# Loading q, and the first two batches of k, as rows of eight tokens, in a kernel of windowed attention followed by an expert layer

## The chip, the cores and the metric

The kernel runs on one core of a Trainium2 chip. The metric is the device time of one execution in microseconds (us); less is better. Granted TensorE clock, the share of full speed that the profile shows, is given where it is not near 1. Times of different series come from different chips, so the time of an experiment is compared only with runs of the kernel before on the same chip in the same rounds. Of the kernel before only one profile was kept, so starts and stages in the experiments' profiles are set against that one, across chips.

In the lines of the profile PE is TensorE, PEld its weight loads, DVE VectorE, ACT ScalarE, POOL GpSimd and SP SyncE; L304 is line 304 of that kernel; the span runs from the start to the end of the profiled execution.

## The reference

Attention over 8 batches of 8 heads, 576 tokens, head size 64. A token sees the tokens at most 32 away and 8 global tokens; the global tokens see and are seen by all. Its output goes through a two-matrix layer with a sine activation, called "expert layer" here.

```python
scores = scale * np.matmul(q, k.transpose(0, 1, 3, 2))          # [8, 8, 576, 576]
mask = np.abs(pos[:, None] - pos[None, :]) <= 32
mask = mask | is_global[:, None] | is_global[None, :]
attn = softmax(np.where(mask, scores, -1e9))                     # cut: written out
x = np.matmul(attn, v).transpose(0, 2, 1, 3).reshape(4608, 512)

h = x @ w_in                                                     # [4608, 2048]
s = np.sin(alpha * h)
out = (h + s * s / (alpha + 1e-09)) @ w_out                      # [4608, 512]
```

## The kernel before

All work of a batch is one attention stage and one expert stage; in the steady state the second half of the expert layer of batch b-1 fills the attention stage of batch b, and the loads of batch b+1 are issued there too. Batch 0 has nothing to be overlapped with: its attention is the *front* of the program.

Loads of q, k and v and of the weights are issued by GpSimd, which casts to bf16 on the way. One load of q or k is one head (the first two batches, `split`) or one tile of 96 tokens; a piece of it is one token of one head, 64 elements, 256 bytes in DRAM and 128 bytes as bf16.

```python
def load_slots(b, split):
    QS = qkp.tile([TW, NTW, H, D], BF, name="QS")     # 96 x 6 x 8 x 64
    KS = qkp.tile([TW, NTW, H, D], BF, name="KS")
    ...                                                # cut: by_head, by_tile, v_rows
    f = by_head if split else by_tile
    kq = [partial(f, src, dst, i) for i in range(H if split else NTW)
          for src, dst in ((k, KS), (q, QS))]
    ...
    return kq[:4] + vs + kq[4:] if split else kq + vs
```

Both are transposed two heads at a time on TensorE into PSUM (six transposes of 96 columns each), and copied out: k by VectorE, laid out window by window (overlapping windows, 1344 elements per partition), q by ScalarE.

The front also needs small things: the rows of the global tokens (`gN`, gathered by SyncE's and ScalarE's queues, k first, then q, then v), a copy of global v into the buffer of v (`VgN` to `VW`), and the vector alpha, brought with its elements spread over the partitions.

The start of the main program, in order:

```python
stage_T(0, 0, psA, "qp"); globals_all(); ...; stage_T(0, 1, psA, "qp")
globals_v_all()                        # cast of global v, then the reciprocal
shift_v(0)                             # SyncE: shifted copies of v
global_v(0)                            # SyncE: VW<-VgN, waits for the cast
parts, last = attention(0, psA, {2: 0, 3: 2})
with_extra(parts, w_loads, 3, 2)       # GpSimd: 8 weight loads, 2 per attention step
parts[3] = partial(chain, parts[3], pool_regs)
late = load_slots(1, True)             # issued in batch 0's expert stage
```

GpSimd takes a weight load when it comes to it.

The softmax here doesn't subtract the row's maximum and nothing guards it: scores larger than these inputs give would overflow.

## Time and profile before

| | before |
|---|---|
| time, median of 3 runs | 385.82 us (385.81 to 385.98) |
| span of the profiled run, granted clock | 385.0 us, 0.996 |
| first attention output matmul (`num`) | 29.27 us |
| first expert matmul (`hb`) of batch 0 / batch 1 | 46.29 / 90.68 us |
| between later batches | 37.97 to 38.48 us |

The page of the profile of before, from the slices of the span (one digit is the busy tenths of 9.6 us), the packet count and the shares of the chain that ended last:

```profile
PE   1128499798999999999999999999999999999796
DVE  7725459574977497649774976497749774954500
...
DMA packets 133723, 35.31 MB, mean 92 GB/s; under 512 B 123314, under 2 KB 128178, under 8 KB 133682
...
PE 52%; ACT 18%; DVE 10%; issue 7%; POOL 7%; DMA 3%; POOLq 1%; ACTq 0%; DVEq 0%
```

From the ninth slice on TensorE is the limit (8 or 9 tenths nearly to the end). In the first five it is not: there TensorE is at 1, 1, 2, 8, 4 tenths and something else holds the program. The stage table of before confirms this. Its columns are the stretch, its length, then busy us (and instructions) of PE, PEld, DVE, ACT and POOL, then the granted clock, the DMA share in tenths and GB/s; the stretches run from one batch's first `hb` matmul to the next one's, for batches 0, 1 and 4:

```profile
46.29:90.68 44.39, 39.97 (x385) 18.53 (x385) 28.59 (x73) 32.83 (x57) 23.88 (x44) 1.00 1.07 106
90.68:128.80 38.12, 37.41 (x384) 18.14 (x384) 26.90 (x64) 32.51 (x57) 31.20 (x53) 1.00 1.65 136
205.63:243.60 37.97, 37.15 (x385) 18.05 (x384) 26.63 (x59) 29.58 (x50) 31.28 (x48) 1.00 0.94 98
```

A steady batch is 37 us of TensorE in 38 us. Batch 0's stage has 4.4 us of TensorE idle time, the front far more.

The timeline of the front in before, VectorE first. Columns: start, length, engine, line, operation, out<-in, shapes, count, and in brackets the idle time before it and what ended that:

```profile
19.99 0.41 DVE L278 CAST VgN<-gN 64x512 bf16<-64x512 f32 x1
25.36 0.25 DVE L279 RECIPROCAL recipT<-alphaT 128x16 f32<-128x16 f32 x1 [4.96 <-DMA alphaT<-in_moe_alpha_dram]
25.52 0.86 DVE L344 TENSOR_TENSOR E<-E,MASK 128x672 bf16<-128x672 bf16 x2
```

The same stretch on TensorE:

```profile
18.54 0.64 PE L304 MATMUL Kps<-identb,KS 96*128 96x96 bf16 x6 [2.27 <-DMA KS<-in_k_dram]
...
29.27 0.58 PE L375 MATMUL num<-E,VW 128*64 128x56 bf16 x12 [2.36 <-DMA VW<-VgN]
...
46.29 16.56 PE L457 MATMUL hb<-xT,w_in 128*128 128x512 bf16 x64 [3.36 <-POOL xT L402]
```

And on GpSimd, the issue of the weights:

```profile
21.79 0.78 POOL L532 DMA_DIRECT2D w_in<-in_moe_w_in_dram  x1 [0.36 <-DMA KS<-in_k_dram]
25.82 0.74 POOL L532 DMA_DIRECT2D w_in<-in_moe_w_in_dram  x1 [3.25 <-DMA QS<-in_q_dram]
32.13 1.49 POOL L532 DMA_DIRECT2D w_in<-in_moe_w_in_dram  x2 [5.56 <-issue]
33.60 2.98 POOL L532 DMA_DIRECT2D w_out<-in_moe_w_out_dram  x4
```

VectorE stands 4.96 us on alphaT and only then does the first mask product, although its input was finished on ScalarE at 22.76. TensorE then still waits for global v (2.36 us). The first weight load is issued at 21.79, and the second only at 25.82, after 3.25 us in which it waits for q's loads.

The groups by form, with busy time, mean ns of one, and idle time before, for the two copies that the change turns into strided ones:

```profile
L310 DVE COPY kTw<-Kps 128x1344 bf16<-128x1344 bf16 x32 | 27.1, 848 | 1.9 <-PE Kps L304 1.9
L324 ACT COPY qT<-qp 128x576 bf16<-128x576 bf16 x20 | 12.7, 633 | 18.4 <-PE ops L268 13.2 <-PE qp L319 5.1
```

### The profile page before, as it was taken

The numbers are of one execution on the slowest core, as the hardware profiler recorded it, in microseconds if no ns is written. First come the engines' busy times: TensorE is split into PE (matmuls) and PEld (weight loads), VectorE is DVE, ScalarE is ACT, GpSimd is POOL, SyncE is SP. The second block draws the span as 40 slices with busy tenths as digits, with TensorE's granted clock in tenths as the row PEclk, the third lists the DMA queues.
The fourth block names the chain that finished last, engine by engine and source line by source line (L and its number), as shares of the span: only waits on it lengthen the run. The fifth ranks groups of instructions, "written<-read, shape, count | busy, mean of one in ns | idle before, by whom it ended". The sixth has DMA issues, their size and how long they took to land.

```text
span 385.0 us, 8609 instructions
## 1 busy us (share of the span) xinstructions
PE 336.2 (87%) x3208; PEld 162.9 (42%) x3208; DVE 244.9 (64%) x551; ACT 258.4 (67%) x435; POOL 249.3 (65%) x394
## 2 busy tenths in 40 slices
PE   1128499798999999999999999999999999999796
PEld 0015244443444444444544444444444444344342
DVE  7725459574977497649774976497749774954500
ACT  1057487786988588858885888578857885744310
POOL 8934396227878589858986898689768006854400
PEclk9999999999999999999999999999999999999989
DMA  6999999257999409940994099409940001000012
GB/s 53 136 162 161 190 164 165 37 77 77 155 132 153 124 9 103 148 127 7 103 148 126 7 103 149 128 6 113 137 128 5 30 30 54 2 28 27 29 54 82
DMA packets 133723, 35.31 MB, mean 92 GB/s; under 512 B 123314, under 2 KB 128178, under 8 KB 133682
## 3 DMA queue, kind: packets, MB, share of 16 engines
q0 software_dynamic: 122560, 19.02, 69.4%
q1 hardware_dynamic: 8034, 15.54, 13.9%
q10 hardware_dynamic: 3088, 0.21, 0.8%
q8 instruction: 25, 0.41, 0.4%
q14 instruction: 16, 0.13, 0.1%
HBM read 38.42 MB, written 9.44 MB: 124 GB/s over the span
## 4 chain that ended last, share of the span: by engine, by line
PE 52%; ACT 18%; DVE 10%; issue 7%; POOL 7%; DMA 3%; POOLq 1%; ACTq 0%; DVEq 0%
PE hb L457 22%; PE ops L494 13%; PE o L494 8%; ACT Sb L464 6%; ACT E L342 4%; DMA KS<-in_k_dram 3%; DVE H2b L447 3%; PE num L375 3%; ACT S L470 2%; DVE S L472 2%; DVE kTw L310 2%; ACT lnd L358 2%; PE hb L494 2%; ACT rec L360 2%; PE Sp L336 2%
## 5 line engine op out<-in xcount | busy, mean ns | idle before, releaser
L457 PE MATMUL hb<-xT,w_in 128*128 128x512 bf16 x576 | 133.1, 384 | 6.0 <-POOL xT L402 4.8
L464 ACT ACTIVATE Sb<-hb,alphaT 128x512 bf16<-128x512 f32 x144 | 96.6, 684 | 55.2 <-PE hb L457 53.9
L447 DVE SCALAR_TENSOR_TENSOR H2b<-S,recipT,hb 128x512 bf16<-128x512 bf16 x144 | 102.6, 741 | 29.3 <-POOL S L472 28.8
L472 POOL TENSOR_TENSOR S<-Sb 128x512 bf16<-128x512 bf16 x91 | 92.6, 1040 | 34.1 <-ACT Sb L464 31.5
L457 PEld LDWEIGHTS <-w_in 128*128 128x128 bf16 x576 | 56.5, 99 | 74.4 <-issue 10.9
L494 PE MATMUL ops<-w_out,H2b 128*128 128x512 bf16 x320 | 81.7, 385 | 3.2 <-DVE osb L502 3.0
L494 PEld LDWEIGHTS <-H2b 128*128 128x128 bf16 x576 | 50.6, 98 | 58.6 <-issue 7.3
L344 DVE TENSOR_TENSOR E<-E,MASK 128x672 bf16<-128x672 bf16 x64 | 34.1, 534 | 32.9 <-ACT E L342 32.2
L494 PE MATMUL o<-w_out,H2b 128*128 128x512 bf16 x224 | 54.7, 380 | 0.0
L342 ACT ACTIVATE E<-Sp 128x672 bf16<-128x672 f32 x64 | 45.9, 717 | 4.1 <-PE Sp L336 4.0
L402 POOL COPY xT<-xg 128x4 bf16 x64 | 12.9, 201 | 48.9 <-DVE xg L400 45.5
L107 POOL DMA_DIRECT2D VW<-in_v_dram x56 | 42.5, 776 | 0.7 <-issue 0.3
L358 ACT ACTIVATE lnd<-den 128x288 f32<-128x288 f32 x64 | 26.4, 412 | 18.3 <-PE den L352 17.8
L382 DVE TENSOR_TENSOR xT<-num,rec 128x288 bf16<-128x288 f32 x64 | 28.7, 449 | 6.1 <-PE num L375 4.8
L375 PEld LDWEIGHTS <-VW 128*64 128x64 bf16 x768 | 18.3, 116 | 33.1 <-DVE gn L386 10.9
L472 DVE TENSOR_TENSOR S<-Sb 128x512 bf16<-128x512 bf16 x30 | 18.3, 609 | 21.5 <-ACT Sb L464 20.6
L375 PE MATMUL num<-E,VW 128*64 128x56 bf16 x768 | 25.3, 201 | 6.9 <-DVE gn L386 3.1
L360 ACT ACTIVATE rec<-lnd 128x288 f32<-128x288 f32 x64 | 28.3, 443 | 2.0
L310 DVE COPY kTw<-Kps 128x1344 bf16<-128x1344 bf16 x32 | 27.1, 848 | 1.9 <-PE Kps L304 1.9
L336 PE MATMUL Sp<-qT,kTw 64*128 64x56 bf16 x768 | 22.1, 190 | 6.0 <-ACT E L342 4.1
L100 POOL DMA_DIRECT2D QS<-in_q_dram x30 | 23.2, 774 | 3.0 <-DMA QS<-in_q_dram 3.0
L324 ACT COPY qT<-qp 128x576 bf16<-128x576 bf16 x20 | 12.7, 633 | 18.4 <-PE ops L268 13.2
(73 smaller groups left out, 305.1 us busy)
## 6 DMA issues: line engine op xcount, KB each, us to landing
out_dram<-osb SPq DMA_DIRECT2D x36, 256.0 KB
VW<-in_v_dram POOLq DMA_DIRECT2D x40, 112.0 KB, 4.8
VW<-VW SPq DMA_DIRECT2D x8, 384.0 KB
KS<-in_k_dram POOLq DMA_DIRECT2D x30, 96.0 KB, 4.7
QS<-in_q_dram POOLq DMA_DIRECT2D x30, 96.0 KB, 4.7
w_in<-in_moe_w_in_dram POOLq DMA_DIRECT2D x4, 512.0 KB, 8.0
w_out<-in_moe_w_out_dram POOLq DMA_DIRECT2D x4, 512.0 KB, 13.1
VW<-VW SPq DMA_DIRECT2D x8, 240.0 KB
```

The source lines that it names most:

```text
L107: nc.gpsimd.dma_start(out=W[p0 : p0 + n, par, u, :].rearrange("p (h d) -> p h d", d=D), in_=v[b, :, key0 : key0 + n, :].rearrange("h p d - ...
L310: nc.vector.tensor_copy(out=kTw[hp][:, :, 0:KB], in_=bass.AP(tensor=base.tensor, offset=base.offset, ap=[list(base.ap[0]), [QB, NW], [1, KB]],
L342: nc.scalar.activation(out=E[:], in_=Sp[:, :, 0:EW], func=AF.Exp, scale=scale)
L344: nc.vector.tensor_tensor(out=E[:], in0=E[:], in1=mk[:, None, :].to_broadcast([P, 2, EW]), op=ALU.mult)
L358: nc.scalar.activation(out=lnd[:], in_=den[:, :, 0:QB], func=AF.Ln)
L360: nc.scalar.activation(out=rec[:], in_=lnd[:], func=AF.Exp, scale=-1.0)
L375: nc.tensor.matmul(out=num[pr, u, :], lhsT=W[:, i % 2, i // 2, c0 : c0 + 64], rhs=E[:, t, u * QC : (u + 1) * QC], start=True, stop=True, s ...
L447: nc.vector.scalar_tensor_tensor(out=H2b[:, n_, :], in0=s_[:], scalar=recipT[:, n_ : n_ + 1], in1=h_, op0=ALU.mult, op1=ALU.add,)
L457: nc.tensor.matmul(out=h2[:], lhsT=w_in[:, ci, nt * P : (nt + 1) * P], rhs=xT[:, ci, c * CH : (c + 1) * CH], start=(ci == 0), stop=(ci == ...
L464: nc.scalar.activation(out=Sb[:], in_=h2[:], func=AF.Sin, scale=alphaT[:, nt : nt + 1])
L472: eng.tensor_tensor(out=S2[:], in0=Sb[:], in1=Sb[:], op=ALU.mult)
L494: nc.tensor.matmul(out=ops[:], lhsT=H2b[:, nt, ts * P : (ts + 1) * P], rhs=w_out[:, nt, :], start=(nt == 0), stop=(nt == NT - 1),)
```

## The change

The intent: eight consecutive tokens of one head lie side by side in DRAM, 2 KB in one piece. If a partition takes eight tokens of one head, the loads have an eighth of the pieces and, with several heads per load, there are fewer loads to issue. The tokens then stand on 72 partitions, eight to a partition, so the transposes are of one head at a time (72 columns, 16 in place of 6), write tokens in the order "j, then partition", and the copies out of PSUM read with a stride to put them back. All q, and k of batches 0 and 1, go this way. With GpSimd freed of issues, half the squares of the first expert stage and all of the second's go to the later split, in which GpSimd does most of them.

```diff
-        QS = qkp.tile([TW, NTW, H, D], BF, name="QS")
-        KS = qkp.tile([TW, NTW, H, D], BF, name="KS")
+        QS = qkp.tile([TR, H, JR, D], BF, name="QS")                 # 72 x 8 x 8 x 64
+        KS = qkp.tile([TR, H, JR, D] if b < 2 else [TW, NTW, H, D], BF, name="KS")
...
-        f = by_head if split else by_tile
-        kq = [partial(f, src, dst, i) for i in range(H if split else NTW) for src, dst in ((k, KS), (q, QS))]
+        n_ = 2 if split else H
+        if b < 2:
+            kq = [partial(by_rows, src, dst, i, n_) for i in range(0, H, n_) for src, dst in ((k, KS), (q, QS))]
+        else:
+            kq = [partial(by_tile, k, KS, i) for i in range(NTW)] + [partial(by_rows, q, QS, 0, H)]
...
+        if b < 2:
+            for j in range(JR):
+                for t, pr in heads:
+                    nc.tensor.transpose(
+                        out=Kps[pr, j * RP + WR : j * RP + WR + TR],
+                        in_=KS[:, 2 * hp + t, j, :], identity=identb[0:TR, 0:TR])
+            nc.vector.tensor_copy(
+                out=kTw[hp][:, :, 0:KB].rearrange("p i (c j) -> p i c j", j=JR),
+                in_=kview([[QB // JR, NW], [1, KB // JR], [RP, JR]]))
...                                                    # q alike, in every batch
         nc.scalar.copy(
-            out=qT[hp][:, :, 0:QB], in_=Qps[:].rearrange("p (i c) -> p i c", c=QB)
+            out=qT[hp][:, :, 0:QB].rearrange("p i (c j) -> p i c j", j=JR),
+            in_=Qps[:].rearrange("p (j i c) -> p i c j", j=JR, c=QB // JR),
         )
...
+    sq_first = lambda nt: (sq_early if nt < 8 else sq_late)(nt)
...
-                        ld = load_slots(p + 1, p == 1)
+                        ld = load_slots(p + 1, False)
                         if p == 1:
-                            late = ld[5:]
-                            ld = ld[:5]
-                            with_extra(parts, ld, 6, 1)
+                            with_extra(parts, ld, 3, 2)
...
-            m1 = mm1(p, H2[p], psB, sq_early if p < 2 else sq_late)
+            m1 = mm1(p, H2[p], psB, sq_late if p else sq_first)
```

More of the change, by code (lines that the diff above doesn't have):

```diff
@@ L52 @@
     NTW = S // TW
+    JR = 8
+    TR = S // JR
+    WR = WIN // JR
+    RP = TR + 2 * WR
     CT = DM // P
@@ L88, in load_slots, with by_rows @@
     def load_slots(b, split):
-        QS = qkp.tile([TW, NTW, H, D], BF, name="QS")
-        KS = qkp.tile([TW, NTW, H, D], BF, name="KS")
+        QS = qkp.tile([TR, H, JR, D], BF, name="QS")
+        KS = qkp.tile([TR, H, JR, D] if b < 2 else [TW, NTW, H, D], BF, name="KS")
         qk[b] = (QS, KS)
         W = VW[b % 2]
-        def by_head(src, dst, h):
+        def by_rows(src, dst, h0, n):
             nc.gpsimd.dma_start(
-                out=dst[:, :, h, :], in_=src[b, h].rearrange("(t p) d -> p t d", p=TW)
+                out=dst[:, h0 : h0 + n, :, :].rearrange("p h j d -> p h (j d)"),
+                in_=src[b, h0 : h0 + n].rearrange("h (p j) d -> p h (j d)", j=JR),
             )
@@ L299, in globals_in @@
         )
+    heads = [(t, slice(64 * t, 64 * t + 64)) for t in range(2)]
     def stage_T(b, hp, qpool, qtag):
         QS, KS = qk[b]
-        for jt in range(NTW):
-            nc.tensor.transpose(
-                out=Kps[:, WIN + jt * TW : WIN + (jt + 1) * TW],
-                in_=KS[:, jt, 2 * hp : 2 * hp + 2, :],
-                identity=identb[0:TW, 0:TW],
-            )
-        base = Kps[:, 0:1]
-        nc.vector.tensor_copy(
-            out=kTw[hp][:, :, 0:KB],
-            in_=bass.AP(
-                tensor=base.tensor, offset=base.offset,
-                ap=[list(base.ap[0]), [QB, NW], [1, KB]],
-            ),
-        )
@@ L317, in stage_T, with kview @@
-        Qps = qpool.tile([P, S], BF, name=qtag)
-        for jt in range(NTW):
-            nc.tensor.transpose(
-                out=Qps[:, jt * TW : (jt + 1) * TW],
-                in_=QS[:, jt, 2 * hp : 2 * hp + 2, :],
-                identity=identb[0:TW, 0:TW],
-            )
+        base = Kps[:, 0:1]
+        def kview(ap):
+            return bass.AP(tensor=base.tensor, offset=base.offset, ap=[list(base.ap[0])] + ap)
+        if b < 2:
[3 more added lines that the diff above has]
+                        out=Kps[pr, j * RP + WR : j * RP + WR + TR],
+                        in_=KS[:, 2 * hp + t, j, :],
+                        identity=identb[0:TR, 0:TR],
+                    )
+            nc.vector.tensor_copy(
+                out=kTw[hp][:, :, 0:KB].rearrange("p i (c j) -> p i c j", j=JR),
+                in_=kview([[QB // JR, NW], [1, KB // JR], [RP, JR]]),
+            )
+        else:
+            for jt in range(NTW):
+                nc.tensor.transpose(
+                    out=Kps[:, WIN + jt * TW : WIN + (jt + 1) * TW],
+                    in_=KS[:, jt, 2 * hp : 2 * hp + 2, :],
+                    identity=identb[0:TW, 0:TW],
+                )
+            nc.vector.tensor_copy(
+                out=kTw[hp][:, :, 0:KB],
+                in_=kview([[QB, NW], [1, KB]]),
+            )
@@ L324, in stage_T @@
+        Qps = qpool.tile([P, S], BF, name=qtag)
+        for j in range(JR):
+            for t, pr in heads:
+                nc.tensor.transpose(
+                    out=Qps[pr, j * TR : (j + 1) * TR],
+                    in_=QS[:, 2 * hp + t, j, :],
+                    identity=identb[0:TR, 0:TR],
+                )
         nc.scalar.copy(
-            out=qT[hp][:, :, 0:QB], in_=Qps[:].rearrange("p (i c) -> p i c", c=QB)
+            out=qT[hp][:, :, 0:QB].rearrange("p i (c j) -> p i c j", j=JR),
+            in_=Qps[:].rearrange("p (j i c) -> p i c j", j=JR, c=QB // JR),
@@ L326, in stage_T @@
         )
     EW = NU * QC
-    heads = [(t, slice(64 * t, 64 * t + 64)) for t in range(2)]
     def stage_Q(psA, b, hp, hf):
```

## The prediction

> **What bounds the kernel now.** From the first expert matmul of batch 1 on (line hb, 90.7 us) TensorE sets the pace: the stage table gives 13.2 us busy of 13.7 and about 24.1 of 24.8 in alternate stretches, so one batch takes 38.2 us; The front is different: hb starts only at 46.3 us. The timeline shows why: keys of heads 2-3, issued at 12.7 behind all of v, are transposed at 18.5; VectorE idles 5.0 us until alphaT lands (25.4); TensorE idles until the global v rows land (29.3), their transfer having been issued at 20.4 behind 12 more q/k loads. After that eight attention steps of about 2 us run on latency. In the first expert stage ScalarE alternates sine and square (1.81 us per two tiles, against 1.73 on TensorE), so its tail is late: the last H2b ends at 66.7.
>
> **What the change does.**
> 1. Front. 16 q/k loads of 576 pieces become 8 of 144. At 0.72 us each GpSimd saves 5.8 us of issue, and heads 2-3 come with the first four. In its fullest 2 us the DMA moved 2400 of the 128-byte packets (154 GB/s) against 400 of the 1024-byte ones (205 GB/s), so bytes move only about 1.3 times faster, not 8 times. I expect global v usable near 24-25 us instead of 29.3: -4 to -5 us. Given back: the copy to kTw. It now runs 1344 bf16 in 0.85 us, two elements a cycle; the Trainium skill (VectorE: DVE Perf Modes, "What auto-detection actually checks") wants step 1 for that, and 0.85 us fits. With step 80 I expect one per cycle, about 1.5 us: +0.65 us each, eight times, partly exposed in the front: +1. Net -3.5 us.
> 2. First expert stage. GpSimd is free after eight tiles, so squares leave ScalarE; the tail ends about 1.5 us earlier; slow kTw copies at the switch to batch 1 take back 0.6. Net -1.
> 3. Batch 1's expert stage loses its loads and uses GpSimd squares. It took 15.55 us on TensorE, the same as later stages: about 0.
> 4. Steady batches. The six 96-column q transposes (0.26 us warm) become 16 of 72 columns with half-width output. The num matmuls, alternating halves likewise, run 12 in 0.21 us, 17.5 ns each at 56 columns; an estimate of 18-23 ns gives 0.29-0.37 us. At four a batch on a full TensorE: +0.1 to +0.45 us per batch, about +2 us over seven. The q copy on ScalarE (0.63 us) now reads PSUM in strides; I expect 0.63-0.8, +0.3 us in all. Five saved DMA issues a batch are worth nothing.
>
> Sum: -3.5 -1 +2.3 = about -2.3 to -4. **Predicted 382.6 us, range 378.0 to 386.5**; faster by over 2%: 0.10; within 2%: 0.88; slower by over 2%: 0.02.
>
> **What would show it.** hb's first matmul at 41.5-44 us; DMA wait on global v mostly gone; kTw copies near 1.5 us for batches 0 and 1, 0.85 after; 16 q transposes 0.29-0.37 us; period 38.3-38.7 us; POOL busy far lower; packets 133,700 down to about 93,000.
>
> **What would make it wrong.** The weight loads, now issued about 6 us earlier, may crowd alphaT and global v, so that they land no sooner (front gains only 1). Transposes of the two halves may not overlap: 33 ns each, +0.27 us per stage, +7 us in all, no gain. Strided PSUM reads may slow the ScalarE copy to over 1 us.

## More of the kernel before

```python
for i, src in enumerate((k, q, v)):
    for eng, js in halves:                             # nc.sync: 4 tokens, nc.scalar: 4 tokens
        for j in js:
            eng.dma_start(out=gN[i][j : NG * B : NG, :]..., in_=src[:, :, bass.ds(regs[j], 1), :]...)
nc.scalar.dma_start(out=alphaT[:], in_=moe_alpha.rearrange("(t p) -> p t", p=P))
...
def globals_v_all():
    nc.vector.tensor_copy(out=VgN[:], in_=gN[2][:])
    nc.vector.reciprocal(out=recipT[:], in_=alphaT[:])
```

In that `rearrange` neighbours in the destination are 128 elements apart in DRAM, so the load is 2048 pieces of 4 bytes. The reciprocal is wanted first in the expert stage. It stands ahead of the attention's mask products in VectorE's program.

## The result and the profile after

A ratio here is of the runs of one kernel over those of before, with its 95% interval; it is not quite the ratio of the medians quoted. Executions over 1.5% slower than the fastest of the same kernel are left out of the means.

| | before | after |
|---|---|---|
| time, median (4 runs each) | 385.82 us | 400.49 us (398.82 to 401.46) |
| ratio, 95% interval | | 1.0366 (1.0336 to 1.0395): slower |
| span of the profiled run, granted clock | 385.0 us, 0.996 | 398.3 us, 0.996 |
| first `num` | 29.27 | 38.03 |
| first `hb` of batch 0 / batch 1 | 46.29 / 90.68 | 56.68 / 103.02 |
| between later batches | 37.97 to 38.48 | 38.29 to 38.55 |

The page of after (a slice is now 10 us):

```profile
PE   1202659879899999999999999999999999999796
DVE  7901736967496749755965696478748864853500
...
DMA packets 94526, 35.36 MB, mean 89 GB/s; under 512 B 78354, under 2 KB 88978, under 8 KB 94482
...
PE 55%; issue 12%; ACT 10%; DVE 10%; POOL 8%; DMA 3%; POOLq 1%; ACTq 0%; DVEq 0%
```

The packets fell as intended. But in the third slice both TensorE and VectorE stand at 0, where before they had 2. The shares of the chain, which add up the whole span, do not point there; the timeline does. VectorE of after:

```profile
21.46 0.42 DVE L286 CAST VgN<-gN 64x512 bf16<-64x512 f32 x1 [1.78 <-DMA gN<-in_v_dram]
36.55 0.25 DVE L287 RECIPROCAL recipT<-alphaT 128x16 f32<-128x16 f32 x1 [14.67 <-DMA alphaT<-in_moe_alpha_dram]
36.72 0.85 DVE L369 TENSOR_TENSOR E<-E,MASK 128x672 bf16<-128x672 bf16 x2
```

TensorE of after; `den` is the first matmul that takes a masked E:

```profile
37.22 0.49 PE L377 MATMUL den<-E,ones 128*64 128x336 bf16 x2 [15.61 <-DVE E L369]
...
38.03 0.53 PE L400 MATMUL num<-E,VW 128*64 128x56 bf16 x12
...
42.71 0.46 PE L361 MATMUL Sp<-qT,kTw 64*128 64x56 bf16 x12 [1.24 <-DVE kTw L326]
...
56.68 16.49 PE L482 MATMUL hb<-xT,w_in 128*128 128x512 bf16 x64 [3.37 <-POOL xT L427]
```

GpSimd of after:

```profile
15.35 1.57 POOL L557 DMA_DIRECT2D w_in<-in_moe_w_in_dram  x2
22.12 1.49 POOL L557 DMA_DIRECT2D w_in<-in_moe_w_in_dram  x2 [5.20 <-issue]
23.59 2.99 POOL L557 DMA_DIRECT2D w_out<-in_moe_w_out_dram  x4
```

VectorE stands 14.67 us on alphaT in place of 4.96, TensorE 15.61 us on VectorE, and there is no wait for global v left to be seen, because it ended inside the longer one. The weights are issued from 15.35 on, two at once, in place of 21.79, one at a time; the last four from 23.59, in place of 33.60. The first moves by 6.4 us, the others by about 10, since the wait of 3.25 us for q's loads is gone as well.

The stage table of after, same columns and the same batches as before:

```profile
56.68:103.02 46.34, 40.30 (x465) 18.95 (x465) 31.39 (x71) 31.11 (x53) 31.09 (x51) 1.00 1.06 114
103.02:141.31 38.29, 37.89 (x425) 18.43 (x425) 25.92 (x58) 29.64 (x50) 27.57 (x43) 1.00 0.80 97
218.15:256.44 38.29, 37.89 (x425) 18.44 (x424) 26.63 (x59) 29.65 (x50) 27.58 (x43) 1.00 0.80 97
```

The copies of after, by form; the eight strided ones are those of batches 0 and 1:

```profile
L326 DVE COPY kTw<-Kps 128x1344 bf16<-128x1344 bf16 x8 | 12.4, 1550 | 0.5 <-PE Kps L321 0.5
L337 DVE COPY kTw<-Kps 128x1344 bf16<-128x1344 bf16 x24 | 20.3, 846 | 0.0
L349 ACT COPY qT<-qp 128x576 bf16<-128x576 bf16 x20 | 12.7, 633 | 18.5 <-PE ops L276 13.8 <-PE qp L344 4.7
```

Where the 13.36 us between the two profiled runs (398.33 less 384.97) lie, from the starts of `hb`:

| stretch | before | after | difference |
|---|---|---|---|
| start to first `hb` of batch 0 (front) | 46.29 | 56.68 | +10.39 |
| to first `hb` of batch 1 | 44.39 | 46.34 | +1.95 |
| to first `hb` of batch 7 (six batches) | 229.32 | 230.00 | +0.68 |
| to the end | 64.97 | 65.31 | +0.34 |

Three quarters are in the front. The steady part, which the change touches in every batch, is nearly the same.

### What alphaT meets in the DMA engines

The trace has a record for every piece that moved. Counted by queue in stretches of 2 us:

```
            stretch    4-byte pieces, ScalarE's queue    beside them, GpSimd's queue
before      18 to 20   1653                              881 of 128 bytes
after       26 to 28   321                               316 of 1024 bytes
after       30 to 32   403                               388 of 1024 bytes
after       32 to 34   406                               390 of 1024 bytes
```

Half of alphaT's pieces had moved at 19.3 us in before and at about 30 in after; the last at 24.8 and 36.5. In these stretches the 4-byte queue got one piece for each piece of 1024 bytes (those of the weights): some 200 in a microsecond, so its 2048 need at least 10 us (an estimate: 2048 over 403 in 2 us), though they are only 8 KB. The Trainium skill (DMA: Bandwidth & Descriptors, "Queues, rings and completion order") says that each DMA engine takes turns between the queues that have work, a packet at a time. The near-equal counts beside the weights would follow from such turns if a turn moved as many pieces of either queue, which the records do not show; beside 128-byte ones the counts were not equal (1653 to 881). Nor is the slowing the weights' alone: in before some 390 of the 2048 were left at 20 us and took until 24.8, in the stretch (19.1 to 24.8) in which the 112 pieces of 5 and 6 KB of v's shifted copies moved. In after the first 350 or so, from 21.3 to 26, went beside those and the weights. That alphaT is 2048 pieces at all is as the same page's "Rules for kernel authors" has it: a strided last dimension becomes one descriptor per element.

### The profile page after: what moved, and what is told of

Read it like the earlier page. It is cut to its first block, busy times and chain, and to the rows that moved or that the text cites. A ratio compares the mean times of both kernels' runs of the same rounds, so it can differ in the third digit from the quotient of the medians.

```text
span 398.3 us, 9366 instructions
## 1 busy us (share of the span) xinstructions
PE 340.7 (86%) x3608; PEld 166.4 (42%) x3608; DVE 247.5 (62%) x543; ACT 254.0 (64%) x424; POOL 232.2 (58%) x363
## 2 busy tenths in 40 slices
DMA packets 94526, 35.36 MB, mean 89 GB/s; under 512 B 78354, under 2 KB 88978, under 8 KB 94482
## 4 chain that ended last, share of the span: by engine, by line
PE 55%; issue 12%; ACT 10%; DVE 10%; POOL 8%; DMA 3%; POOLq 1%; ACTq 0%; DVEq 0%
PE hb L482 24%; PE ops L519 15%; PE o L519 7%; DVE H2b L472 3%; ACT E L367 3%; DVE S L497 3%; PE num L400 3%; ACT Sb L489 2%; DVE kTw L337 2%; DMA KS<-in_k_dram 2%; PE hb L519 2%; PE Sp L361 2%; ACT lnd L383 2%; POOL VW L112 2%; ACT rec L385 1%
## 5 line engine op out<-in xcount | busy, mean ns | idle before, releaser
L489 ACT ACTIVATE Sb<-hb,alphaT 128x512 bf16<-128x512 f32 x144 | 97.6, 686 | 59.9 <-PE hb L482 58.1
L497 POOL TENSOR_TENSOR S<-Sb 128x512 bf16<-128x512 bf16 x110 | 111.7, 1040 | 39.3 <-ACT Sb L489 36.6
L369 DVE TENSOR_TENSOR E<-E,MASK 128x672 bf16<-128x672 bf16 x64 | 32.3, 506 | 32.9 <-ACT E L367 32.9
L377 PE MATMUL den<-E,ones 128*64 128x336 bf16 x128 | 21.6, 331 | 15.6 <-DVE E L369 15.6
L105 POOL DMA_DIRECT2D KS<-in_k_dram x36 | 27.9, 790 | 0.0
L497 DVE TENSOR_TENSOR S<-Sb 128x512 bf16<-128x512 bf16 x22 | 16.4, 746 | 17.5 <-ACT Sb L489 16.6
L361 PEld LDWEIGHTS <-kTw 64*128 64x128 bf16 x768 | 15.7, 96 | 21.8 <-issue 15.1
```

The lines of the kernel that those rows point to most:

```text
L361: nc.tensor.matmul(out=Sp[:, t, u * QC : (u + 1) * QC], lhsT=kTw[hp][pr, i, :], rhs=qT[hp][pr, i, :], start=True, stop=True, skip_group_ch ...
L369: nc.vector.tensor_tensor(out=E[:], in0=E[:], in1=mk[:, None, :].to_broadcast([P, 2, EW]), op=ALU.mult)
L489: nc.scalar.activation(out=Sb[:], in_=h2[:], func=AF.Sin, scale=alphaT[:, nt : nt + 1])
L497: eng.tensor_tensor(out=S2[:], in0=Sb[:], in1=Sb[:], op=ALU.mult)
```

## The experiments

The theory after the result: the loss in the front is one wait, of VectorE on alphaT; alphaT is late because the weight loads come about 6 us sooner and share the DMA engines with its 2048 pieces; the rest is the slow k copy (twice in the front, twice at the switch to batch 1). The rivals: the row loads themselves, whose pieces are large, crowd alphaT; the 16 transposes and strided copies cost more than their trace lines show; global v was pushed back as well, so that removing alphaT's wait gains nothing.

### Series 1 (before on the same chip: 386.53 us, 384.21 to 387.82, 7 runs)

**e1_after_alpha_first**: after, with alphaT loaded ahead of the gathers.

```diff
     nc.scalar.dma_start(out=gcol[KB : KB + NG, :], in_=global_idx[:, None])
+    nc.scalar.dma_start(out=alphaT[:], in_=moe_alpha.rearrange("(t p) -> p t", p=P))
...
-    nc.scalar.dma_start(out=alphaT[:], in_=moe_alpha.rearrange("(t p) -> p t", p=P))
```

> The kernel after the change, with the alphaT load (2048 pieces of 4 bytes) issued on ScalarE's queue ahead of the gathers of the global rows instead of behind them. Theory (the 4-byte alphaT load crawls beside the 1 KB packets of the weight loads): alphaT lands long before it is needed, the 14.7 us wait of VectorE goes, the first mask product starts near 21.5 us; the front is then held by the global v rows, whose packets ran at 26 to 30 us, so the first num matmul comes near 30 to 31 us instead of 38.0, the first hb matmul near 49 instead of 56.7, and the time near 393 us. Rival (the front is slow because of the one-head transposes and strided copies, alphaT is a bystander): time stays at 399 to 401 us.

Measured 391.57 us (390.93 to 392.29), ratio 1.0127 (1.0077 to 1.0178). The reciprocal no longer waits (21.18); `num` starts at 29.85, now after 7.13 us on global v, `hb` at 48.31, 8.37 sooner than in after.

```profile
29.85 0.59 PE L400 MATMUL num<-E,VW 128*64 128x56 bf16 x12 [7.13 <-DMA VW<-VgN]
```

Batch 0's stage took 46.74, the later ones 38.28 to 38.75. Some two thirds of the loss was alphaT's lateness. The rest is elsewhere.

**e2_before_alpha_first**: the same edit on before.

> The kernel before the change, with the same early alphaT load. VectorE's wait of 5.0 us for alphaT goes, but the global v rows landed at 29.3 us, so if they are the next limit the first num moves by at most about 1 us and the time is 384.5 to 386 us. If alphaT alone held the front, hb would start some 3.5 us earlier and the time would be near 382.

Measured 386.72 us (386.38 to 387.54), ratio 1.0011 (0.996 to 1.0061), just above what was expected. The reciprocal ran at 21.68, and `num` at 30.19, after 5.11 us on global v, 0.9 later than without the edit. So in before alphaT's wait was covered by that for global v. The edit gains nothing by itself; what it gains in e1 is the change's own damage.

**e3_after_weights_later**: after, with 7.7 us of dummy work on GpSimd ahead of the weight loads.

```diff
                     global_v(0)
+                    for _ in range(11):
+                        nc.gpsimd.iota(PAD[:], pattern=[[1, S]], base=0, channel_multiplier=0)
                     parts, last = attention(0, psA, {2: 0, 3: 2})
```

> The kernel after the change, with about 6 us of useless work (11 iotas into a scratch tile) on GpSimd between the last q/k load of batch 0 and the first weight load, so that the weight loads are issued at about 21 us again, as before the change; the row loads, transposes and copies stay. Theory (the weight loads moved earlier and crowd the small packets): alphaT lands by about 25 us, global v by about 27 us, hb starts near 45 to 47 us instead of 56.7, time near 389 us. Rival (the 1 KB packets of the row loads of q and k themselves hold alphaT up, or the transposes do): alphaT still lands beyond 32 us and the time stays over 395 us.

Measured 389.37 us (388.29 to 392.47), ratio 1.0092 (1.0022 to 1.0162). The weights were issued at 23.29, 30.43 and 31.89; GpSimd's first of them and VectorE of this run:

```profile
23.29 1.54 POOL L558 DMA_DIRECT2D w_in<-in_moe_w_in_dram  x2
...
24.26 0.25 DVE L288 RECIPROCAL recipT<-alphaT 128x16 f32<-128x16 f32 x1 [1.44 <-DMA alphaT<-in_moe_alpha_dram]
```

The alphaT load is untouched, the row loads are all there, and alphaT lands at 24.26 in place of 36.55. So it is not the row loads that crowd it, but the weight loads. (The gathers of the global rows may lose something to the row loads: their last piece landed at 20.4 here and at 19.0 in before.) `num` starts at 27.84, 1.4 us sooner than in before, `hb` at 46.38, the same as in before: the slower k copies use up the 1.4. Making GpSimd *slower* took the loss from 3.7% of before's time to 0.9%.

**e4_before_weights_sooner**: before, without any row load; the four `w_in` loads are issued ahead of the q and k loads of heads 4 to 7, at 15.59 to 18.6 us.

```diff
-    for f in ld0[4:]:
+    for f in ld0[4:15]:
+        f()
+    WG = DFF // 4
+    for i in range(4):
+        nc.gpsimd.dma_start(out=w_in[:, :, i * WG : (i + 1) * WG], in_=moe_w_in[...]...)
+    for f in ld0[15:]:
         f()
...
-                    with_extra(parts, w_loads, 3, 2)
+                    with_extra(parts, w_loads[4:], 3, 2)
```

> The kernel before the change, q and k loaded in 256-byte pieces, transposed and copied as before, but with the four w_in loads issued ahead of the q/k loads of heads 4 to 7, at about 15.5 to 18 us. Theory: alphaT now shares the DMA engines with 1 KB packets and lands near 28 to 30 us instead of 25.4, global v near 31 instead of 29.3; hb starts 2 to 5 us later and the time is 388 to 391 us, without any row load in the kernel. Rival (only the row loads or transposes of the change are slow): alphaT stays at 25 us and the time at 386 us within 1.

Measured 393.19 us (392.3 to 394.01), ratio 1.0175 (1.0122 to 1.0228), more than expected. GpSimd and VectorE:

```profile
15.59 3.03 POOL L201 DMA_DIRECT2D w_in<-in_moe_w_in_dram  x4
...
32.72 0.25 DVE L287 RECIPROCAL recipT<-alphaT 128x16 f32<-128x16 f32 x1 [12.30 <-DMA alphaT<-in_moe_alpha_dram]
```

`num` at 34.21, `hb` at 51.83. The damage can be had without any part of the change, by moving the weights forward. Of `hb`'s 5.5 us, 4.9 stand before `num`; the late heads 4 to 7 account at most for the 0.6 that follow.

### Series 2 (before on the same chip: 385.59 us, 383.86 to 386.74, 11 runs)

**e5_q_rows_steady_only**: before, with q as rows from batch 2 on only: one row load a batch, among the k loads, 16 transposes and the strided ScalarE copy.

```diff
+        if b > 1:
+            kq = [partial(f, k, KS, i) for i in range(H if split else NTW)]
+            kq.insert(4, partial(by_rows, q, QS))
...
+        if b > 1:
+            for j in range(JR):
+                for t, pr in heads:
+                    nc.tensor.transpose(...)           # as in the change
+            nc.scalar.copy(...)                        # as in the change
+            return
```

> The kernel before the change, in which only q of batches 2 to 7 is loaded by rows (one load of 576 pieces of 2 KB), transposed head by head (16 transposes of 72 columns) and put in order by the ScalarE copy; batches 0 and 1, the weight loads and the squares stay. This is the steady part of the change alone. Theory (it costs the TensorE time of the longer transposes, about 0.1 us each, and nothing else): a batch takes about 0.10 to 0.15 us longer, 38.34 us instead of 38.24 between first hb matmuls, the time rises by 0.6 to 1 us (386.4 to 386.8), the q copy stays at 0.63 us. Rival 1 (fewer packets help steady batches): 384 to 385.5 us. Rival 2 (the transposes of the two halves do not overlap): + 0.27 us a stage, 391 us or more.

Measured 396.59 us (394.03 to 399.19), ratio 1.0276 (1.0238 to 1.0314): a miss, and by the experiment's own build. With `split`, the list goes first four, then all of v, then the rest; the one load of batch 2's q fell behind v, was issued at 95.70 and had to bring all heads before the first transpose:

```profile
109.07 0.69 PE L334 MATMUL hb<-identb,QS 72*64 72x72 bf16 x16 [8.26 <-DMA QS<-in_q_dram]
```

That profile also has 6.8 us of halved granted clock in that stretch (mean 0.981; other runs of it 0.983 to 0.996). The total says nothing of the steady cost, but the five batches after it do: 38.28 to 38.34 us each, where the least of before is 37.97. That is 0.31 more, about double the 0.10 to 0.15 expected.

**e6_after_alpha_first_k_old**: e1, and k loaded and transposed as in before, so only q is in rows.

```diff
-            kq = [partial(by_rows, src, dst, i, n_) for i in range(0, H, n_) for src, dst in ((k, KS), (q, QS))]
+            kq = []
+            for i in range(0, H, 2):
+                kq += [partial(by_head, k, KS, i), partial(by_head, k, KS, i + 1), partial(by_rows, q, QS, i, 2)]
...
-        if b < 2:                                      # in stage_T, for k
+        if False:
```

> The kernel of the first experiment (after the change, alphaT loaded first), with k of batches 0 and 1 loaded in 256-byte pieces by head, transposed six at a time and copied with unit steps as before; q stays in rows. Theory (the strided copies to kTw, 1.55 us instead of 0.85, cost their difference wherever the next transposes wait for Kps): from first hb of batch 0 to first hb of batch 1 it is about 44.6 us instead of 46.7, first num to first hb in batch 0 about 17 us instead of 18.5, time about 388 us against 391.6 of the first experiment. Rival (the two stages are slower because of the moved squares and the moved loads of batch 2): the stretch stays at 46.7 us and the time over 390.

Measured 393.06 us (390.81 to 393.22), ratio 1.0201 (1.0172 to 1.0231). One part as expected: from `num` to `hb` 17.05 us, as in before (17.02), against 18.46 in e1. So k by rows costs the front 1.4 us, which is what its two strided copies take more (1550 less 846 ns each). The other part missed: batch 0's stage took 46.35, not some 44.6. There are now 19 loads in the first expert stage, and the change's GpSimd squares stand behind them; TensorE shows

```profile
62.99 1.02 PE L489 MATMUL hb<-xT,w_in 128*128 128x512 bf16 x4 [1.27 <-DVE H2b L479]
```

Its runs had clocks of 0.983 to 0.996, so part of the total is not the edit's.

**e7_before_front_mended**: before, with alphaT first, global v's copy on ScalarE's queue, and the weight loads held by a one-element GpSimd copy that reads global v's place.

```diff
-        nc.sync.dma_start(
+        (nc.sync if b else nc.scalar).dma_start(                   # global_v
...
+    nc.scalar.dma_start(out=alphaT[:], ...)                        # moved up, as in e1
...
                     global_v(0)
+                    pool_regs()
+                    nc.gpsimd.tensor_copy(out=gate[96:128, :], in_=VW[0][96:128, 0, 0, 0:1])
```

> The kernel before the change with the front mended and no row loads: alphaT loaded first on ScalarE's queue, global v of batch 0 sent on ScalarE's queue instead of behind the two shifts on SyncE's, GpSimd's register loads moved ahead of the weight loads, and the weight loads held back until global v of batch 0 has landed (a one-element GpSimd copy reads it). If the small packets' company is what sets the front, global v lands near 24 to 26 us instead of 29.3, hb starts near 42 to 43.5 us and the time is 382 to 383.5 us. If the weights, now issued near 25 us, come too late for the first expert stage, hb stalls and the time is 386 or more.

Measured 386.23 us (384.5 to 387.6), ratio 1.0016 (0.9985 to 1.0047). A miss: `num` at 29.52. With alphaT ahead on ScalarE's queue the gathers behind it came late, and the cast of global v ran at 24.50 in place of 19.99. Here the small load that was put first made another one late.

**e8_after_front_mended**: the same on after.

> The kernel after the change with the same mended front. With the crowding gone, what the change itself is worth shows: about 7 us less than with alphaT alone mended, global v near 24 us, hb near 43 us, then the strided copies (+2 us up to batch 1) and longer transposes (+1 us) remain: 385 to 386.5 us, some 3 us slower than the mended kernel before the change. If row loads are worth something in the front once nothing crowds them, it comes within 1 us of that kernel.

Measured 393.06 us (391.57 to 395.57), ratio 1.0215 (1.018 to 1.0249), clocks 0.977 to 0.996. A miss in the total. `num` is at 28.11 and `hb` at 46.58, so the front is down to before's, but batch 0's stage took 47.31.

### Series 3 (before on the same chip: 386.29 us, 384.27 to 387.85, 11 runs)

**e9_after_reciprocal_late**: after, with one instruction moved, and no DMA touched: VectorE's reciprocal goes behind the attention of batch 0.

```diff
     def globals_v_all():
         nc.vector.tensor_copy(out=VgN[:], in_=gN[2][:])
-        nc.vector.reciprocal(out=recipT[:], in_=alphaT[:])
...
                 run(parts + [last], counts + [0], fill)
+                if p == 0:
+                    nc.vector.reciprocal(out=recipT[:], in_=alphaT[:])
```

> The kernel after the change with one instruction moved: VectorE's reciprocal of alphaT, which waits for the alphaT load, comes after the attention of batch 0 instead of ahead of its first mask product. No transfer is issued elsewhere or in another order; alphaT itself still lands near 36 us. Theory (the front lost its time in VectorE's queue behind that one wait): the first mask product comes near 22 us instead of 36.7, the first num waits for global v near 29 to 31 us instead of 38.0, first hb near 48 to 49.5 us instead of 56.7, time near 392 us, as with alphaT loaded first. Rival (the crowded DMA engines hold up all of the front, the global v rows too, until the weights are in): first num stays beyond 35 us and the time over 397.

Measured 392.52 us (391.84 to 393.37), ratio 1.0157 (1.0112 to 1.0202), as expected. VectorE and TensorE of this run:

```profile
21.47 0.42 DVE L286 CAST VgN<-gN 64x512 bf16<-64x512 f32 x1 [1.84 <-DMA gN<-in_v_dram]
21.82 0.91 DVE L368 TENSOR_TENSOR E<-E,MASK 128x672 bf16<-128x672 bf16 x2
```

```profile
31.11 0.59 PE L399 MATMUL num<-E,VW 128*64 128x56 bf16 x12 [7.86 <-DMA VW<-VgN]
...
49.54 0.58 PE L481 MATMUL hb<-xT,w_in 128*128 128x512 bf16 x1 [3.35 <-POOL xT L426]
```

The first mask product follows the cast at once (21.82, not 36.72), while alphaT comes as late as ever (its last piece at 36.9). So the place of the reciprocal in VectorE's program was the cost, and it is worth 7.14 us of `hb` (56.68 less 49.54). Only 7, not 15, since global v comes next, at 31.11. That is 1.84 *later* than in before: the weights crowd it too.

**e10_before_mended_again**: before with the late reciprocal, alphaT issued behind global v on SyncE's queue, and the gate of e7 for the weights.

```diff
-    nc.scalar.dma_start(out=alphaT[:], ...)
...
                     global_v(0)                                     # on nc.scalar, as in e7
+                    nc.sync.dma_start(out=alphaT[:], in_=moe_alpha.rearrange("(t p) -> p t", p=P))
+                    pool_regs()
+                    nc.gpsimd.tensor_copy(out=gate[96:128, :], in_=VW[0][96:128, 0, 0, 0:1])
```

> The kernel before the change with its front mended otherwise than in the seventh experiment, where loading alphaT first had pushed the gathers of the global rows back (the cast of the gathered v rows came at 24.5 us instead of 20.0): alphaT is loaded last, on SyncE's queue behind the shifts, its reciprocal follows the attention of batch 0; global v of batch 0 goes on ScalarE's queue; GpSimd's register loads stand ahead of the weight loads, and those wait for global v. If the chain gather, cast, global v sets the front, the cast comes at 20 us again, global v lands near 25 to 26.5 us instead of 29.3, first hb near 42.5 to 44 us, time 382 to 384 us: it beats both kernels by under 1%. If not, 385 to 387 us.

Measured 386.17 us (383.77 to 387.3), ratio 1.0002 (0.9968 to 1.0036): a miss. The cast ran at 20.75 and the copy of global v was issued at 21.20, but its pieces moved only from about 26 us on, though the weights were held; `num` at 29.08 after 3.25 us on it. Why the copy stood for over 4 us is not settled; by then three quarters of alphaT's pieces, issued before it at 17.80 on SyncE's queue, had moved, and no run tests whether the one held up the other.

**e11_after_mended_again**: the same on after.

> The kernel after the change with the same mended front as the tenth experiment. Global v should land near 25 to 27 us, first hb near 44 to 45.5 us; the rest of the change (strided k copies, about 2 us up to batch 1, and 0.3 us more a batch of TensorE transposes) stays: 387 to 389.5 us, 4 to 6 us slower than the tenth experiment. If it comes within 2 us of it, the row loads do pay in the front and my account of the remainder is wrong.

Measured 391.8 us (390.04 to 393.34), ratio 1.0131 (1.0089 to 1.0174), above the expectation. `num` at 27.78 and `hb` at 46.23; but batch 0's stage was 50.31 in a profile whose granted clock was halved for 10 us of it (mean clock of the runs 0.983 to 0.996). The front is as good as before's, the total cannot be read finely.

**e12_k_old_squares_old**: e6 with before's split of the squares in the first expert stage.

```diff
-            m1 = mm1(p, H2[p], psB, sq_late if p else sq_first)
+            m1 = mm1(p, H2[p], psB, sq_late if p else sq_early)
```

> The sixth experiment (after the change, alphaT first, k of batches 0 and 1 loaded, transposed and copied as before) with the squares of batch 0's first expert stage on ScalarE and VectorE as before the change. In the sixth, 19 loads took GpSimd's first ten slots of that stage and its squares waited behind them (TensorE idled 1.3 us for H2b). Theory (strided copies and nothing else make the stretch from first hb of batch 0 to first hb of batch 1 longer than before the change): it falls from 46.35 to 44.3 to 44.9 us, against 44.39 before the change, and the time to about 389 us. Rival (the moved loads of batch 2 or the q rows cost there too): it stays over 45.5 us.

Measured 390.56 us (389.12 to 391.71), ratio 1.0105 (1.0058 to 1.0153). Batch 0's stage is 44.47 us, before's 44.39: with old k copies and old squares its whole loss is gone. The parts of what is left, against before's profile (another chip), add up: front +1.45 (`hb` at 47.74), batch 0's stage +0.08, six batches +2.04 (231.36 less 229.32), end +0.36, together 3.93 us, as the spans have it (388.9 less 385.0).

### Series 4 (before on the same chip: 386.18 us, 384.45 to 387.02, 11 runs)

**e13_before_v_gathered_first**: before, with the late reciprocal, global v gathered first in place of last, and its cast and copy put ahead of the shifts of v.

```diff
-    for i, src in enumerate((k, q, v)):
+    for i, src in ((2, v), (0, k), (1, q)):
...
                     stage_T(0, 0, psA, "qp")
+                    globals_v_all()
+                    global_v(0)
                     globals_all()
...
-                    globals_v_all()
                     shift_v(0)
-                    global_v(0)
```

> The kernel before the change with no transfer added, only reordered: the global rows of v are gathered ahead of those of k and q, cast and copied into the v windows ahead of the two shifts; the reciprocal of alphaT follows the attention of batch 0. Theory (once alphaT is out of VectorE's way, the chain gather of v, cast, copy of global v is the front's limit): global v lands by 22 to 24 us instead of 29.3, the first num comes when its mask product does, at 24 to 26 us, first hb near 42 to 43.5 us, time 382 to 383.5 us. Rival (the front is held by the whole load of the DMA engines, whatever the order): first num stays near 29 us and the time at 385 to 387 us.

Measured 383.6 us (382.86 to 386.11), ratio 0.994 (0.9917 to 0.9962). `num` begins at 25.58, as meant, and then stops:

```profile
25.58 0.26 PE L374 MATMUL num<-E,VW 128*64 128x56 bf16 x2
28.53 0.47 PE L374 MATMUL num<-E,VW 128*64 128x56 bf16 x10 [2.69 <-DMA VW<-VW]
```

The shifted copies of v are the next limit, and they are there only 0.7 us sooner than global v was in before (28.53 against 29.27); so `hb` is at 45.44, not at 42 to 43.5. The profile is of its slowest run, 386.11 us; the five others took 382.86 to 384.51. This is the one version that beats both kernels, by 0.6%, and it has nothing of the change in it.

**e14_after_v_gathered_first**: the same on after.

> The same reordering in the kernel after the change, whose weight loads still go out at 15.4 us. Theory: alphaT, late as before, no longer matters; global v lands before the weights crowd it, the first num comes near 24 to 26 us, first hb near 42.5 to 44.5 us; then the slower k copies and q transposes of the change remain: 386 to 388 us, 3 to 5 us slower than the thirteenth experiment. Rival (the weights sent at 15 us delay the shifts and global v whatever their order): first num 29 us or later and 390 us or more.

Measured 388.62 us (387.83 to 390.71), ratio 1.0082 (1.0054 to 1.011). All of it lies a little above the expectation: `num` at 26.88, `hb` at 45.30. By the profiles both fronts are alike now (45.44 in e13), though e13's profile is of a run 2.5 us slower than its median. The rest of the change still costs 5.0 us by the medians (388.62 less 383.6). The two profiles show 2.1 of them, 1.27 in batch 0's stage (45.79 against 44.52) and most of the remainder after it, where the least batch is 38.28 against 37.97; the other 3 are not in this pair, since e13's profile is of its slowest run and e14's (388.21) of an ordinary one.

## Why the prediction was wrong

The prediction said 382.6 us, with 2% for slower by over 2%; the change is slower by 3.7%.

1. **The step that failed: the front.** It read "I expect global v usable near 24-25 us instead of 29.3: -4 to -5 us", and with the copies "Net -3.5 us". The front became 10.39 us longer. The step counted the 5.8 us of GpSimd's issue time as a gain. What GpSimd did with them was to issue the weights 6.4 us sooner (15.35 against 21.79), and this delayed both of the small loads on which the front waits: alphaT from 25.36 to 36.55, global v (as e9 shows it) from 29.27 to 31.11. e4 made the delay without the change, e3 removed it with the change in place. Nor was the gain there to be lost: in e3, with the row loads and the weights held to 23.29, `num` comes at 27.84, after 2.03 us on global v: 1.4 us sooner than in before, not 4 to 5. The prediction set its lateness down to the q and k loads ahead of it. The records of before show its pieces, issued at 20.42, moving from 26.3 on, after the last of v's shifted copies (24.8), which stand ahead of it in SyncE's queue; in e13, where it stands ahead of them, it was in at 20.0. The 10.39 consist of 7.14 for the wait on alphaT (e9), 1.84 for global v, and 1.41 for k by rows, its two strided copies (18.43 us from `num` to `hb` in e9, 17.02 in before, 17.05 in e6 and e12).
2. **The danger was named, and mis-sized.** "The weight loads, now issued about 6 us earlier, may crowd alphaT and global v [...] (front gains only 1)". The mechanism is this one; the size was taken as a lost gain, not as a loss. Two things in before's own trace would have pointed to it: the reciprocal stands ahead of all of the attention on VectorE, so alphaT's delay is passed on to the last microsecond once it is beyond global v's, which was only 4 us away; and alphaT is 2048 pieces. How slowly these move beside pieces of 1024 bytes, no run before the prediction had shown.
3. **The first expert stage: said -1, was +1.95.** The step was "GpSimd is free after eight tiles", and the tail was to end "about 1.5 us earlier"; the last H2b was 20.12 us behind the first `hb`, against 20.43: 0.3 earlier. GpSimd was still issuing the loads of batch 1 until 67.7 us, so its squares, of 1.04 us each, started at 68.19, over 11 us into the stage. The slow copies cost more than the 0.6 put down: from the first scores of batch 1 to its `hb` 23.13 us against 21.79, so 1.35 for the two inside, and 22.03 in e6, where k is old. The remaining 0.6 stand before those scores: on VectorE the first two slow copies are next behind the stage's last H2b. e12, with both parts undone, is back at 44.47 of 44.39.
4. **Batch 1's expert stage: right.** About 0 said; the stretch from its `hb` to the next is 38.29 against 38.12, no more than the steady difference.
5. **The steady batches: right in size.** Said +0.1 to +0.45 us each. The least batch is 38.28 or 38.29 in the kernels with q in rows (but for one of 38.08 in e11) and 37.97 or 37.98 in those without, so +0.31. In the profiled pair the sum of six is only +0.68, as before has batches of 38.4 among those of 37.97, whose cause was not looked for. The 16 q transposes took 0.36 to 0.38 us from their start to that of the next instruction (75.11 to 75.47, 112.86 to 113.24), the six of before 0.26 (77.66 to 77.92):

```profile
77.66 0.42 PE L319 MATMUL qp<-identb,QS 96*128 96x96 bf16 x6
77.92 1.03 PE L494 MATMUL ops<-w_out,H2b 128*128 128x512 bf16 x4
```

```profile
75.11 0.43 PE L344 MATMUL qp<-identb,QS 72*64 72x72 bf16 x16
75.47 1.90 PE L519 MATMUL ops<-w_out,H2b 128*128 128x512 bf16 x8
```

One after the other they would take some 33 ns each (an estimate: 0.26 us over six, times 72 over 96 columns). At 23 ns each the halves do overlap, as the Trainium skill (TensorEngine Tiling (Array Packing), "Key Properties") has it for tiles of half width.
6. **The copies: right.** kTw 1550 ns (1.5 us said), as the rule of step 1 in the Trainium skill (VectorE: DVE Perf Modes, "What auto-detection actually checks") let expect, against 846 ns where the old layout stays. The ScalarE copy, "0.63-0.8", was 633 ns, no slower at all with strides. The packets are 94,526 (about 93,000 said).

So the terms that the prediction took from durations in the trace (copies, transposes, period) held. The two that hang on what GpSimd does with the time it saves (the weights in the front, the squares in the first expert stage) did not: the prediction did not follow GpSimd's program to what comes next.

What stays open: why global v's copy stood for over 4 us in e10; the lower granted clock of several kernels in series 2 and 3; the scatter of some 0.4 us between steady batches; and whether the row loads shorten the front at all: with the same repair of the order of things the profiles show the same front (45.30 in e14, 45.44 in e13), but 3 us between the medians of that pair are not placed.

## What to carry to other kernels

When a change relieves an engine that issues loads, ask which loads it will issue sooner, and what they will meet: here 6 us saved on GpSimd moved the weights into the one moment at which two small loads held the program. An instruction that waits for a late load should stand in its engine's program where its result is wanted, not where the load is declared; moving one reciprocal was worth 7 us. And a load of thousands of 4-byte pieces is to be counted in pieces, not in bytes: here 8 KB in 2048 pieces took from 21.3 to 36.5 us beside the weights.

## What the Trainium skill lacked or had wrong

- DMA: Bandwidth & Descriptors, "Queues, rings and completion order": the turns between queues are there, but not what a queue of tiny pieces gets beside large ones. Here 403 pieces of 4 bytes moved in 2 us beside 388 of 1024 bytes, and 1653 beside 881 of 128 bytes. The page speaks of whole packets of several descriptors per turn; the records of these runs show no packet bounds, so they neither confirm nor contradict that.
- The same page, "Rules for kernel authors": the row on a strided last dimension holds, but has no price. Here an 8 KB vector issued at about 16 us landed at 25.36 us, and at 36.55 beside earlier weight loads.
- The same page, "Measured (HBM→SBUF, 128 partitions, SWDGE, issued from GpSimd)": the table goes by the size of a load, not of its pieces, and the page's part on small descriptors has no measured rate for loads from HBM. Pieces of 128 bytes moved at 154 GB/s (2400 in 2 us, counted as written), pieces of 1024 bytes at 205 GB/s (400 in 2 us), so an eighth of the pieces was only 1.3 times faster. Its rule to batch loads has a price as well: the 576 KB row load of q landed 9.6 us after issue by the median, the 96 KB loads of k after 4.0, and nothing of it could be used before (8.26 us of TensorE in e5).
- No page gives the cost of a ScalarE copy that reads PSUM with a stride: 633 ns for 128x576 bf16, the same as with step 1.
